# Block-sparse attention followed by a Fourier mixing layer: q and k of the later head pairs turned by VectorE instead of TensorE, with a new order of steps

## The chip, the cores and the metric

One core of one Trainium2 chip runs the whole program. A core has five engines that run side by side, each with its own queue of instructions that it works off strictly in order: TensorE (PE; its weight loads are listed apart as PEld), VectorE (DVE), ScalarE (ACT), GpSimd (POOL) and SyncE (SP). SP issues most of the DMAs, which sixteen DMA engines carry out. Engines wait for each other through semaphores. TensorE writes its results to PSUM, and DVE or ACT bring them to SBUF; GpSimd works only on SBUF here.

The metric is the device time of one execution in microseconds (us), as the median of several runs. A profile is of one execution.

## The reference

For each of 4 batches, 8 heads, 768 positions and head size 64, the program computes an attention in which a query sees its own block of 64 keys and the three blocks whose mean key scores highest, and of these only keys at or before it. The heads are laid side by side to 768 x 512, and a Fourier mixing layer and a two-layer network with W1 (512 x 2048) and W2 (2048 x 512) follow.

```python
k_rep = k.reshape(B, H, n_blocks, block, D).mean(axis=3)          # block 64, 12 blocks
gate_scores = np.einsum('bhsd,bhnd->bhsn', q, k_rep)
gate_scores = np.where(causal, gate_scores, -1000000000.0)
top_idx = np.argsort(gate_scores, axis=-1)[..., -top_k:]          # top_k 3
# mask: the chosen blocks and the query's own block, key position <= query position
scores = scale * np.matmul(q, k.transpose(0, 1, 3, 2))
attn = softmax(np.where(mask, scores, -1000000000.0))
x = np.matmul(attn, v)                                            # then (B, S, H * D)

mixed = np.real(np.fft.fft(np.fft.fft(x, axis=1), axis=2))
u = x + mixed
un = (u - mean(u)) / np.sqrt(var(u) + 1e-06)
out = u + np.maximum(un @ w_ch1, 0.0) @ w_ch2
```

All inputs and the output are float32.

## The kernel before

Two heads make a head pair, P = 0 to 15, four to a batch. A pair's q and k are needed with the head dimension on the partitions: 64 rows of the one head above 64 rows of the other, 768 positions along the free dimension. In DRAM a head is 768 rows of 64 floats. `load` (L264) brings it to SBUF with positions on the partitions, as a tile `nat` of 128 x 6 x 2 x 64, and `a_tp` (L286) lets TensorE transpose the six 128 x 128 blocks into PSUM as the tile `tp`. From there `a_sums` (L294) adds k over blocks of 64, `a_k` (L304) casts k to f16 for the scores, and `a_q32` (L313) copies q to a float32 tile in SBUF.

The code is a set of small steps, and the order in which they are issued is written out as one long list, ORDER (L112 to L179), with each step as name:arguments. The instructions of an engine stand in its queue exactly as their steps stand in this list. The place of a step beside steps of *other* engines has no force of its own: there, only data and buffers make one wait for another. The steps, with their engines:

| step | engine | what |
|---|---|---|
| Lk, Lq, Lv : P | SP | loads of k, q, v of pair P; v is cast to f16 by vc : P (POOL) |
| tk, tq : P | PE | six transposes of k, of q, into `tp` (L292) |
| ks, kh : P | DVE | sums of k by block (L297); the same, kept apart by head |
| kc : P; qc : P; qs : P | ACT; DVE; POOL | k to f16 (two instructions from pair 7 on, L311); q to SBUF (L316); q to f16 (two, L225) |
| g : P | PE | gate scores (L342), from the float32 q and the sums of k |
| gt, gx, gl, gm : P | DVE | gate scores turned (L354), the highest found, compared, and turned back (L386) |
| K : P | POOL | the choice of blocks, as 32 more rows below q (8 instructions, L225, and a memset up to pair 9) |
| s : P,i; e : P,i; d : P,i | PE; ACT; POOL | scores of piece i (L414); exp (L431); the diagonal blocks cut (L437) |
| v : P; x : P | PE; DVE | 42 matmuls with v (L449); divided by the sum, into the batch's `x` |
| fs, fd, f : b or P | DVE | additions that halve the Fourier transform |
| y; ty, tr; m : b | PE; ACT, DVE; PE | Fourier transform along positions (L519), copies out of PSUM, then along the features (L552) |
| u, bn, nv; xu; nr : b | DVE; ACT; POOL | x + mixed, its statistics; centring; the inverse root (12 small instructions) |
| xt, un (batch 0); un (others) | PE, DVE; SP | transposes of the centred rows to `unT`, later by transposing DMAs (L593) |
| w : b,i; r : b,i | PE; ACT, DVE for every fourth i | one of 16 column blocks of W1: eight matmuls (L629, L631); relu (L641, L639) |
| c : b,st,h; o; od | PE; DVE; SP | W2, half of the sum for 128 rows (L656; L648 for the last 128 rows, in halves of 256 columns); added to u (L668); store (L673) |
| W, X; Li, LF, LT, Lc | POOL; SP | loads of W1 in three parts, of W2 in two (X:0, X:1); constants |

The work of one batch's mixing layer is laid beside the attention of the next. "The first W1 product" is the step w of batch 0 that comes first.

Three pools set more waits. PSUM is cut into four buffers of two banks (`pst`, L215); every PE step that makes a new result takes one, and has to wait until the result before it in that buffer has been read. `nat` has three buffers each for q and k, so the load of pair P waits until pair P-3 has been read. The f16 q and k (`qk`) have three slots.

The functions that the diff touches, and what calls them:

Of the kernel before, what the change touches and what calls it, by code (L numbers as in the profile page):

```python
# [183 lines left out]
def kernel(  # L184
# [101 lines left out]
    def a_tp(P, who):  # L286
# [4 lines left out]
        for st in range(NST):  # L291
            nc.tensor.transpose(ps[:, 128 * st:128 * st + 128], src[:, st, :], id32)  # L292
# [495 lines left out]
```

## Time and profile before

| | |
|---|---|
| median of 3 runs | 298.1 us (298.1, 298.16, 297.7) |
| span of the profiled execution, first to last instruction | 295.6 us |
| busy in the span: PE, PEld | 286.5, 180.2 us |
| busy in the span: DVE, ACT, POOL | 192.5, 164.2, 111.1 us |
| DMA packets, data | 93200, 33.53 MB |

The whole time of the profiled execution is not on record apart from its span; the runs beside it took 2.1 to 2.6 us more than that span. Busy time is the time in which an engine has an instruction in work. PE works on several matmuls at once, so the duration of one (a 128 x 512 matmul has a mean of 379 ns) is longer than the time from one to the next; the chain that ended last shows the latter. In rows of groups, `out<-in` names tiles, then come the shapes, the count, the busy time and the mean duration of one in ns, and the idle time of the engine just before them. In the step names used here, the profile's `tp` rows on PE are tk and tq, `h` rows are w, `c` rows are c, `sc` are s, `av` are v.

### The profile page before, as it was taken

The page shows a single profiled execution, that of the slowest core. Times are in us where ns is not written, and L with a number is a line of the kernel's source. Part 1 is how long each engine was busy: PE and PEld are TensorE (multiplying, and loading weights), DVE is VectorE, ACT ScalarE, POOL GpSimd, SP SyncE. Part 2 cuts the span into 40 slices and gives each one's busy share as a digit, 9 for nine tenths or more (in the row PEclk, how much of TensorE's full clock was granted, in tenths as well). Part 3 has the DMA queues.
Part 4 walks back from the last instruction along what each step waited for, and adds up shares of the span by engine and source line. Part 5 has one row for each costly group of instructions (what it writes and reads, how often), then busy time and mean ns, then how long its engine had stood idle before and what let it go on. Part 6 is the DMA issues. An engine that isn't in the chain of part 4 may idle for free.

```text
span 295.6 us, 6738 instructions
## 1 busy us (share of the span) xinstructions
PE 286.5 (97%) x2633; PEld 180.2 (61%) x2633; DVE 192.5 (65%) x597; ACT 164.2 (56%) x205; POOL 111.1 (38%) x286
## 2 busy tenths in 40 slices
PE   8899999999999999999999999999999999999995
...
GB/s 197 268 228 230 262 245 199 195 230 118 226 185 211 168 55 186 118 164 176 3 0 2 0 9 136 38 72 71 2 1 2 32 103 44 142 0 2 0 91 125
DMA packets 93200, 33.53 MB, mean 113 GB/s; under 512 B 85936, under 2 KB 89968, under 8 KB 93168
## 3 DMA queue, kind: packets, MB, share of 16 engines
q1 hardware_dynamic: 87504, 28.47, 40.6%
...
q10 hardware_dynamic: 2000, 0.44, 0.7%
...
q14 instruction: 11, 0.09, 0.1%
...
## 4 chain that ended last, share of the span: by engine, by line
PE 84%; DVE 7%; ACT 6%; DMA 1%; issue 1%; DVEq 0%; ACTq 0%
PE c L656 26%; PE h L629 19%; PE h L631 10%; PE sc L414 7%; PE av L449 6%; ACT pt L431 5%; PE tp L292 5%; PE yp L519 2%; PE mx L552 2%; DVE q L316 2%; PE mx L553 1%; PE warmps L693 1%; DVE u L566 1%; PE g L342 1%; PE c L648 1%; PE sc L409 1%
## 5 line engine op out<-in xcount | busy, mean ns | idle before, releaser
L431 ACT ACTIVATE pt<-sc 128x1024 f16<-128x1024 f32 (+1 forms) x96 | 83.3, 923 | 26.6 <-PE sc L414 19.7
L629 PE MATMUL h<-unT,w 128*128 128x512 f16 x256 | 85.1, 379 | 0.0
L656 PE MATMUL c<-w_sb,hT 128*128 128x512 f16 x368 | 83.8, 379 | 0.0
L631 PE MATMUL h<-unT,w 128*128 128x256 f16 x256 | 69.7, 272 | 0.4 <-DMA unT<-x 0.4
L641 ACT ACTIVATE hT<-h 128x768 f16<-128x768 f32 x48 | 37.8, 813 | 43.7 <-PE h L631 43.7
L656 PEld LDWEIGHTS <-hT 128*128 128x128 f16 x368 | 35.6, 98 | 39.3 <-issue 0.5
L437 POOL TENSOR_SCALAR_AFFINE_SELECT pt<-pt 128x256 f16<-128x256 f16 x96 | 37.5, 414 | 58.5 <-ACT pt L431 57.6
L629 PEld LDWEIGHTS <-w 128*128 128x128 f16 x256 | 25.0, 97 | 29.2 <-issue 1.3
L668 DVE SCALAR_TENSOR_TENSOR u<-c,rs,u 128x512 f32<-128x512 f32 (+1 forms) x25 | 17.5, 725 | 31.2 <-PE c L656 30.4
L639 DVE TENSOR_SCALAR hT<-h 128x768 f16<-128x768 f32 x16 | 15.3, 955 | 29.7 <-PE h L631 29.6
L578 ACT ACTIVATE x<-u,nm 128x512 f16<-128x512 f32 x24 | 15.9, 715 | 22.5 <-DVE nm L572 22.3
L292 PE MATMUL tp<-id,nat 128*128 128x128 f32 x192 | 27.5, 284 | 0.6 <-ACT pt L431 0.3
L631 PEld LDWEIGHTS <-w 128*128 128x128 f16 x256 | 25.0, 98 | 4.3
L225 POOL TENSOR_SCALAR_AFFINE_SELECT qk<-mt 32x160 f16<-32x160 f16 x72 | 23.1, 341 | 10.8 <-DVE mt L386 9.1
L414 PE MATMUL sc<-qk 96*128 96x512 f16 (+3 forms) x144 | 26.8, 305 | 0.0
L225 POOL TENSOR_SCALAR_AFFINE_SELECT qk<-q 64x768 f16<-64x768 f32 (+1 forms) x25 | 20.6, 825 | 14.8 <-DVE q L316 14.1
L292 PEld LDWEIGHTS tp<-id,nat 128*128 128x128 f32 x192 | 22.2, 146 | 5.7 <-issue 1.6
L449 PE MATMUL av<-v,pt 128*128 128x65 f16 x672 | 23.0, 193 | 0.1
L449 PEld LDWEIGHTS <-pt 128*128 128x128 f16 x672 | 22.0, 97 | 1.7 <-POOL pt L437 0.5
L297 DVE TENSOR_REDUCE kr<-tp 128x12 f32<-128x768 f32 x16 | 15.1, 945 | 5.9 <-PE tp L292 5.9
L222 POOL TENSOR_TENSOR t<-vr,rs 128x6 f32<-128x6 f32 x12 | 2.4, 199 | 43.5 <-DVE rs L609 42.9
L414 PEld LDWEIGHTS <-qk 96*128 96x128 f16 x144 | 13.3, 97 | 8.9 <-issue 0.5
...
## 6 DMA issues: line engine op xcount, KB each, us to landing
...
w_sb<-in_moe_w_ch_dram POOLq DMA_DIRECT2D x2, 1024.0 KB, 10.2
...
```

The lines of the kernel that those rows point to most:

```text
L225: nc.gpsimd.affine_select(out=out, in_=in_, pattern=[[0, i] for i in n], base=0, channel_multiplier=0, compare_op=ALU.is_ge, fill=0.0)
L292: nc.tensor.transpose(ps[:, 128 * st:128 * st + 128], src[:, st, :], id32)
L414: nc.tensor.matmul(ps[:, e, co:co + q1 - q0], qk[0:96, e, 1, 128 * jt:128 * jt + 128], qk[0:96, e, 0, q0:q1], start=True, stop=True)
L431: nc.scalar.activation(out=d["pt"][:, o:o + 2 * n].rearrange("p (e c) -> p e c", e=2), in_=d["sc", i][:, :, 0:n], func=AF.Exp, scale=0.125)
L437: nc.gpsimd.affine_select(out=dg, in_=dg, pattern=[[0, 2], [1, 128]], base=0, channel_multiplier=-1, compare_op=ALU.is_ge, fill=0.0)
L449: nc.tensor.matmul(av[:, e, 66 * st:66 * st + 65], pt[:, co:co + 128], vv[:, e, jt, 0:65], start=(cnt == 0), stop=(cnt == 20))
L578: nc.scalar.activation(out=x_b[:, 2 * kp + k2, :], in_=u_b[:, k2, :], func=AF.Identity, scale=0.0625, bias=nm[:, k2:k2 + 1])
L629: nc.tensor.matmul(hp[:, 0:512], w1s, unT[:, dt, 0:512], start=(dt == 0), stop=(dt == NDT - 1))
L631: nc.tensor.matmul(hp[:, 512:768], w1s, unT[:, dt, 512:768], start=(dt == 0), stop=(dt == NDT - 1))
L641: nc.scalar.activation(out=hT, in_=hp, func=AF.Relu)
L656: nc.tensor.matmul(c_ps[b, g[0]][:, st - g[0], :], h_t[b, it][:, 128 * st:128 * (st + 1)], w2_sb[:, it, :], start=(it == 0), stop=(it == N ...
L668: nc.vector.scalar_tensor_tensor(out=o, in0=ps, scalar=st_t[b][1][:, st:st + 1], in1=o, op0=ALU.mult, op1=ALU.add)
```

## The change

For q of pairs 7 to 15 and k of pairs 9 to 15 (`BLK`), the load cuts the head into blocks of 32 positions by 32 features. Four DMAs, one for each head and half of its features, put 32 partitions each: partition r of a group holds position r of each of the 24 blocks, and along the free dimension come the 24 blocks with their 32 features. A DMA's runs are 128 bytes where they were 256. VectorE's 32 x 32 block transpose of that tile, 128 x 768 float32, is then the layout that TensorE made. For q the transpose takes the place of the copy in `a_q32` (qc). For k it is a new step, kb (`k_turn`), which turns the tile in place; `a_sums` and `a_k` then read that SBUF tile. The steps tk:9 to tk:15 and tq:7 to tq:15 are gone, with the PSUM tiles that they wrote, and kb:9 to kb:15 are added.

From w:0 on, the list has a new order: which block of W1 comes when, how scores, W1 and W2 steps alternate on PE, and the queues of ACT, DVE, POOL and SP. Up to there only tq:8 and tq:7 are taken out, and the loads have their new form.

```diff
@@ ORDER @@
...
-e:5,4 m:0,0 u:0,1 xu:0,2 d:5,4 tk:8 d:5,1 d:4,2 u:0,0 xu:0,1 d:5,0 xt:0,2 W:2 g:6 un:0,2 xu:0,0
-xt:0,1 gt:6 tq:8 un:0,1 kc:8 xt:0,0 qc:8 tq:7 un:0,0 qs:8 v:4 Lq:10 Lk:10 Lv:6 Lq:11 qc:7 bn:0,3
-w:0,4 d:5,3 qs:7 bn:0,1 w:0,5 r:0,4 gx:6 ks:8 w:0,6 r:0,5 gl:6,0 kh:7 gl:6,1 x:4 w:0,7 r:0,6 gm:6
-w:0,3 r:0,7 s:6,5 r:0,3 s:6,1 e:6,5 s:6,3 e:6,1 kh:8 s:6,2 fs:4,0 bn:0,4 w:0,2 e:6,2 d:6,1 X:0
-e:6,3 g:7 w:0,0 d:6,5 gt:7 r:0,2 d:6,3 vc:6 gx:7 s:6,4 r:0,0 vc:5 s:6,0 e:6,4 tk:9 Li:0 gl:7,0
-Lv:7 tq:9 gl:7,1 e:6,0 gm:7 w:0,11 Lq:12 Lv:8 K:7 qc:9 kc:9 g:8 r:0,11 v:5 gt:8 d:6,0 ks:9 w:0,8
-qs:9 gx:8 w:0,10 x:5 r:0,8 d:6,4 d:6,2 gl:8,0 s:7,5 s:7,2 r:0,10 kh:9 fs:4,1 w:0,1 bn:0,5 e:7,5
-vc:7 e:7,2 tq:10 gl:8,1 Lv:9 r:0,1 X:1 gm:8 s:7,4 qc:10 w:0,15 d:7,2 e:7,4 K:8 bn:0,0 g:9 r:0,15
-s:7,0 w:0,9 gt:9 e:7,0 gx:9 vc:8 tq:11 r:0,9 d:7,0 Lv:10 s:7,1 qc:11 d:7,5 tk:10 d:7,4 e:7,1
-gl:9,0 s:7,3 ks:10 v:6 e:7,3 kh:10 gl:9,1 kc:10 gm:9 d:7,3 s:8,4 bn:0,2 d:7,1 w:0,12 vc:9 x:6
...
-r:3,12 r:3,9 r:3,14 c:3,0,0 w:3,15 c:3,4,0 r:3,15 c:3,1,0 c:3,0,1 c:3,1,1 c:3,5,0 o:3,0 od:3,0
-o:3,1 c:3,3,0 od:3,1 o:3,5 od:3,5 c:3,4,1 c:3,2,1 o:3,4 od:3,4 c:3,3,1 c:3,5,1 o:3,3 od:3,3 o:3,2
-od:3,2 o:3,6 od:3,6
...
+tr:0,0 s:5,3 d:5,2 s:5,4 d:4,3 kh:6 W:1 ty:0,0 m:0,2 qs:6 e:5,3 u:0,2 m:0,1 vc:4 e:5,4 m:0,0 u:0,1
+xu:0,2 d:5,4 tk:8 d:5,1 d:4,2 u:0,0 xu:0,1 d:5,0 xt:0,2 W:2 g:6 un:0,2 xu:0,0 xt:0,1 gt:6 un:0,1
+kc:8 xt:0,0 qc:8 un:0,0 qs:8 v:4 Lq:10 Lk:10 Lv:6 Lq:11 qc:7 bn:0,3 gx:6 w:0,1 gl:6,0 r:0,1 w:0,2
+gl:6,1 gm:6 r:0,2 w:0,5 s:6,0 s:6,3 w:0,6 ks:8 kh:7 x:4 kh:8 bn:0,4 g:8 g:7 fs:4,1 s:6,1 r:0,5 e:6,0
+e:6,3 r:0,6 gt:7 s:6,4 gx:7 gl:7,0 e:6,4 w:0,0 gt:8 e:6,1 kb:9 ks:9 gl:7,1 gm:7 bn:0,1 r:0,0 w:0,12
+r:0,12 w:0,7 r:0,7 s:6,5 s:6,2 w:0,13 r:0,13 e:6,5 w:0,10 w:0,4 w:0,3 e:6,2 qc:10 gx:8 kb:10 ks:10
+kh:10 qc:9 d:6,1 d:6,4 d:6,0 qs:7 K:7 vc:5 d:6,2 X:0 d:5,3 Li:0 Lv:7 Lq:12 Lv:8 Lv:9 s:7,5 r:0,3
+r:0,4 v:5 x:5 s:7,0 r:0,10 w:0,14 kh:9 gl:8,0 g:9 e:7,5 g:10 e:7,0 gt:9 r:0,14 w:0,8 bn:0,5 gl:8,1
+gm:8 gx:9 fs:5,1 gl:9,0 s:7,4 w:0,15 kc:9 r:0,8 gl:9,1 fs:5,0 gt:10 s:7,3 e:7,4 e:7,3 r:0,15 s:7,1
+e:7,1 w:0,11 r:0,11 gm:9 bn:0,0 bn:0,2 nv:0 s:7,2 kc:10 e:7,2 d:7,5 d:7,0 vc:6 vc:7 K:8 qs:9 d:6,5
+d:6,3 d:7,4 X:1 d:7,1 d:7,2 d:7,3 vc:8 K:9 vc:9 nr:0 Lv:10 Lv:11 Lk:11 w:0,9 r:0,9 v:6 fs:4,0 s:8,4
+s:8,3 x:6 c:0,2,0 c:0,3,0 s:8,1 v:7 c:0,0,0 e:8,4 fs:6,0 x:7 s:8,0 s:9,2 c:0,1,0 s:9,4 c:0,3,1
+fs:6,1 gx:10 fd:6,1 gl:10,0 fd:6,0 gl:10,1 fs:7,1 gm:10 fs:7,0 fd:7,1 fd:7,0 f:1,1 f:1,3 s:8,5 o:0,3
+e:8,3 c:0,1,1 e:8,1 f:1,2 qc:11 o:0,1 s:9,3 e:8,0 e:9,2 s:9,5 c:0,2,1 e:9,4 c:0,0,1 e:8,5 e:9,3
+y:1,1 kb:11 f:1,0 ks:11 kh:11 g:11 y:1,0 e:9,5 o:0,2 s:9,0 o:0,0 ty:1,1 tr:1,1 s:8,2 c:0,4,0 gt:11
+s:9,1 ty:1,0 e:8,2 e:9,0 tr:1,0 m:1,1 Lq:13 od:0,1 Lq:14 od:0,2 od:0,0 Lk:12 Lk:13 qc:12 gx:11
+gl:11,0 gl:11,1 gm:11 u:1,1 e:9,1 m:1,0 u:1,0 m:1,2 kc:11 xu:1,1 xu:1,0 d:8,5 d:8,0 vc:10 vc:11
+d:8,3 qs:10 K:10 d:8,4 d:8,1 qs:11 d:9,4 d:9,2 d:9,5 d:8,2 d:9,0 d:9,1 d:9,3 qs:12 pg:1 K:11 u:1,2
+v:8 v:9 x:8 c:0,5,0 c:0,5,1 xu:1,2 kb:12 s:11,5 s:11,1 e:11,1 x:9 s:10,1 ks:12 kh:12 qc:14 e:10,1
+o:0,5 c:0,4,1 s:10,0 o:0,4 g:12 e:11,5 gt:12 s:11,0 s:10,4 s:11,3 gx:12 bn:1,3 fs:9,0 kb:13 ks:13
+un:1,1 un:1,0 un:1,2 Lk:14 od:0,4 Lv:12 od:0,3 Lv:13 od:0,5 Lk:15 Lq:15 w:1,1 s:10,2 w:1,10 w:1,2
+e:10,0 e:11,0 e:10,4 s:10,3 e:11,3 s:10,5 e:10,2 w:1,11 r:1,10 w:1,8 kh:13 bn:1,0 bn:1,4 kb:14
+gl:12,0 gl:12,1 r:1,1 r:1,2 r:1,11 s:11,4 w:1,7 ks:14 kh:14 qc:13 e:10,3 g:14 kc:13 e:10,5 g:13
+w:1,4 r:1,8 r:1,7 gm:12 e:11,4 kc:12 s:11,2 gt:13 gx:13 gl:13,0 w:1,9 e:11,2 gt:14 w:1,6 fs:8,1
+gx:14 gl:13,1 gm:13 d:10,0 d:10,5 d:10,4 d:10,3 K:12 d:11,0 d:10,2 d:10,1 d:11,3 qs:13 d:11,4 d:11,2
+vc:13 d:11,1 d:11,5 K:13 gl:14,0 r:1,4 v:10 s:12,5 w:1,5 s:12,3 r:1,9 x:10 gl:14,1 r:1,6 w:1,14
+r:1,5 s:12,0 e:12,5 v:11 s:12,2 e:12,3 e:12,0 w:1,0 s:13,2 w:1,3 x:11 kb:15 fs:11,1 fs:8,0 w:1,15
+fs:10,1 fs:9,1 r:1,3 r:1,14 s:13,5 r:1,0 r:1,15 bn:1,1 bn:1,5 fs:10,0 bn:1,2 e:13,2 s:12,1 e:12,2
+w:1,12 s:12,4 e:12,1 w:1,13 r:1,12 kc:15 c:1,0,0 e:13,5 r:1,13 c:1,0,1 s:13,4 s:13,0 e:13,0 c:1,1,0
+fd:10,0 fs:11,0 fd:11,1 fd:11,0 gm:14 fd:10,1 f:2,1 ks:15 kh:15 qc:15 f:2,3 f:2,2 f:2,0 nv:1 e:13,4
+s:13,3 e:13,3 c:1,1,1 s:13,1 e:13,1 e:12,4 d:12,3 d:12,5 K:14 nr:1 d:12,4 d:13,2 d:13,5 qs:14 d:12,2
+qs:15 vc:12 d:12,1 d:13,0 d:13,1 d:13,3 d:12,0 c:1,4,0 o:1,1 y:2,0 tr:2,0 y:2,1 c:1,5,0 o:1,0 g:15
+ty:2,1 tr:2,1 m:2,2 ty:2,0 m:2,0 m:2,1 c:1,4,1 v:12 gt:15 u:2,0 u:2,1 u:2,2 c:1,2,0 c:1,5,1 gx:15
+gl:15,0 gl:15,1 gm:15 kc:14 xu:2,2 xu:2,0 xu:2,1 od:1,1 od:1,0 Lv:14 un:2,2 Lv:15 un:2,1 un:2,0 pg:2
+K:15 d:13,4 s:14,3 o:1,4 e:14,3 c:1,3,0 s:14,0 e:14,0 s:14,4 v:13 s:15,3 c:1,3,1 e:15,3 s:15,0
+s:14,5 s:15,5 e:14,4 e:15,5 c:1,2,1 s:14,2 w:2,3 s:14,1 x:12 o:1,5 e:14,5 s:15,4 bn:2,3 s:15,2
+bn:2,1 bn:2,0 w:2,4 e:15,0 e:14,2 w:2,9 e:15,4 s:15,1 e:15,2 w:2,7 x:13 w:2,2 w:2,1 r:2,4 fs:13,1
+o:1,2 e:14,1 e:15,1 o:1,3 w:2,12 fs:12,1 r:2,3 bn:2,4 bn:2,5 fs:12,0 bn:2,2 nv:2 d:15,0 d:14,2
+d:15,5 d:15,3 d:15,4 vc:15 d:14,5 d:14,3 d:14,0 nr:2 d:14,4 d:15,2 d:15,1 vc:14 d:14,1 v:15 x:15
+r:2,9 r:2,1 v:14 w:2,0 fs:15,0 fs:15,1 w:2,13 w:2,15 x:14 fs:14,0 fs:13,0 r:2,15 w:2,8 r:2,12 w:2,5
+w:2,6 r:2,2 w:2,11 w:2,10 r:2,0 fd:15,1 r:2,7 fs:14,1 fd:14,0 r:2,8 r:2,11 fd:15,0 fd:14,1 f:3,1
+f:3,2 r:2,5 r:2,6 w:2,14 f:3,3 c:2,0,0 r:2,14 r:2,10 c:2,1,0 y:3,1 r:2,13 c:2,0,1 c:2,1,1 tr:3,1
+f:3,0 o:2,0 ty:3,1 y:3,0 ty:3,0 c:2,4,0 tr:3,0 m:3,1 m:3,0 c:2,5,0 m:3,2 c:2,2,0 c:2,2,1 o:2,1 u:3,0
+u:3,1 u:3,2 c:2,4,1 c:2,5,1 bn:3,2 o:2,5 o:2,2 c:2,3,0 c:2,3,1 bn:3,3 bn:3,0 od:1,3 od:1,5 od:2,0
+od:1,2 od:2,1 od:1,4 xu:3,0 xu:3,1 xu:3,2 un:3,0 un:3,2 un:3,1 w:3,15 w:3,4 w:3,14 o:2,3 w:3,6 w:3,2
+r:3,14 w:3,5 w:3,10 r:3,4 r:3,6 o:2,4 r:3,15 bn:3,5 r:3,5 bn:3,1 w:3,0 w:3,8 w:3,7 bn:3,4 r:3,7
+w:3,1 r:3,2 r:3,0 r:3,1 w:3,11 w:3,3 r:3,3 r:3,8 w:3,12 r:3,12 r:3,10 w:3,9 r:3,9 w:3,13 r:3,13
+r:3,11 nv:3 c:3,5,0 c:3,5,1 c:3,0,0 nr:3 pg:3 c:3,1,0 c:3,0,1 c:3,1,1 o:3,0 c:3,2,0 c:3,2,1 o:3,5
+c:3,4,0 c:3,4,1 o:3,6 c:3,3,0 o:3,1 o:3,2 o:3,4 c:3,3,1 o:3,3 od:3,1 od:3,5 od:2,5 od:2,2 od:3,0
+od:2,4 od:2,3 od:3,2 od:3,6 od:3,4 od:3,3
@@ -202,6 +200,7 @@
     NSLOT = 3
     NVS = 4
     NX = 7
+    BLK = (range(7, NPAIR), range(9, NPAIR))
 
     C = _consts_np()
     dr = {n: nc.inline_tensor(C[n], name=f"c_{n}") for n in C}
@@ -258,7 +257,7 @@
 
 
     nat = {}
-    pairs = [{} for _ in range(NPAIR)]
+    pairs = [{"slot": P % NSLOT} for P in range(NPAIR)]
     x_t, u_t, un_t, h_t, st_t = {}, {}, {}, {}, {}
 
     def load(P, who):
@@ -271,10 +270,17 @@
             nat[P, 2] = t
             return
         t = apool.tile([128, NST, 2, 64], FP, tag=f"nat{who}", name=f"nat{who}_{P}", bufs=3)
+        nat[P, who] = t
+        if P in BLK[who]:
+            nat[P, who] = t = t.rearrange("p st e d -> p (st e d)")
+            for g in range(4):
+                eng.dma_start(t[32 * g:32 * g + 32].rearrange("p (n c) -> p n c", c=32),
+                              src[b, 2 * hp + g // 2, :, 32 * (g % 2):32 * (g % 2) + 32]
+                              .rearrange("(n r) c -> r n c", r=32))
+            return
         for e in range(2):
             eng.dma_start(t[:, :, e, :],
                           src[b, 2 * hp + e].rearrange("(st p) d -> p st d", p=128))
-        nat[P, who] = t
 
     def v_cast(P):
         pcopy(v_s[P % NVS][:, :, :, 0:64].rearrange("p e st d -> p (e st) d"), nat[P, 2],
@@ -285,11 +291,14 @@
 
     def a_tp(P, who):
         d = pairs[P]
-        d["slot"] = P % NSLOT
         d["tp", who] = ps = pst([128, S], f"tp{who}_{P}")
         src = nat[P, who].rearrange("p st e d -> p st (e d)")
         for st in range(NST):
             nc.tensor.transpose(ps[:, 128 * st:128 * st + 128], src[:, st, :], id32)
+
+    def k_turn(P):
+        pairs[P]["tp", 1] = t = nat[P, 1]
+        nc.vector.transpose(out=t, in_=t)
 
     def a_sums(P):
         ps = pairs[P]["tp", 1]
@@ -313,7 +322,10 @@
     def a_q32(P):
         q32 = apool.tile([128, S], FP, tag="q32", name=f"q32_{P}")
         pairs[P]["q32"] = q32
-        nc.vector.tensor_copy(out=q32, in_=pairs[P]["tp", 0])
+        if P in BLK[0]:
+            nc.vector.transpose(out=q32, in_=nat[P, 0])
+        else:
+            nc.vector.tensor_copy(out=q32, in_=pairs[P]["tp", 0])
 
     def a_q(P):
         q32, qk = pairs[P]["q32"], qk_s[P % NSLOT]
@@ -737,7 +749,7 @@
         "LT": lambda _: nc.sync.dma_start(fs_sb, dr["FS"].ap()),
         "LF": lambda _: nc.sync.dma_start(fd_sb, dr["FD"].ap()), "Lc": lambda _: consts_next(), "Li": lambda _: ind_slot0(),
         "W": load_w1, "X": load_w2, "iz": blocks,
-        "tk": lambda P: a_tp(P, 1), "tq": lambda P: a_tp(P, 0), "ks": a_sums, "kh": a_half,
+        "tk": lambda P: a_tp(P, 1), "tq": lambda P: a_tp(P, 0), "kb": k_turn, "ks": a_sums, "kh": a_half,
         "kc": a_k, "qc": a_q32, "qs": a_q,
         "g": g_mm, "gt": g_turn, "gx": g_max, "gl": g_less, "gm": g_back, "K": stage_K,
         "s": s_mm, "e": s_exp, "d": s_sel, "vc": v_cast,
```

## The prediction

> **What bounds the kernel now.** I read the granted clock first, then the busy table by stage, PE's own waits, the chain that ended last, and last the rows by shape that price each edit. The busy table has the columns stretch, length, then busy microseconds of PE, PEld, DVE, ACT and POOL, clock, DMA share, GB/s.
>
> ```profile
> core 0: 295.6 us, clock 1.000
> 58.60:100.00 41.40, 41.40 (x423) 26.34 (x420) 35.12 (x137) 29.34 (x36) 24.14 (x53) 1.00 1.02 199
> 100.00:145.00 45.00, 44.62 (x372) 27.98 (x371) 31.95 (x105) 27.38 (x35) 27.25 (x71) 1.00 0.52 121
> 145.00:190.00 45.00, 45.00 (x439) 29.31 (x437) 34.74 (x104) 26.95 (x35) 19.50 (x51) 1.00 0.13 29
> ```
>
> From 58.6 us, where the first W1 product w:0 starts, PE is never free. The waits of PE between 58.6 and 292 us are this one line:
>
> ```profile
> PE h L631 <- DMA unT<-x: 0.4, 1, 0.4
> ```
>
> The chain confirms it: PE's own steps follow each other to the end.
>
> ```profile
> 106.02 0.66 PE tp L292 x6
> 240.21 8.63 PE c L656 x40
> 283.48 6.91 PE c L656 x32
> 290.39 1.76 PE c L648 x16
> 292.17 0.48 DVE u L668
> ```
>
> Forty matmuls of 512 columns in 8.63 us are 0.216 us each, one behind the other, so from 58.6 us on an instruction taken from PE is worth its full issue time, as long as everything else is on time. Before 58.6 us DVE and ACT lead. A w step (eight matmuls) is 1.30 us, a c step 1.73, v 1.28, g 0.41, m 0.87, an s step 0.11 to 0.44.
>
> The rows that price the edit (operation, shapes, count | busy, mean ns | idle before):
>
> ```profile
> L316 DVE COPY q<-tp 128x768 f32<-128x768 f32 x16 | 15.1, 945 | 3.6 <-PE tp L292 3.5
> L349 DVE STREAM_TRANSPOSE gt<-g 128x288 f32<-128x288 f32 x7 | 3.3, 473 | 0.0
> L354 DVE STREAM_TRANSPOSE gt<-g 128x160 f32<-128x160 f32 x9 | 3.1, 346 | 3.5 <-PE g L342 3.4
> L727 POOL DMA_DIRECT2D w_sb<-in_moe_w_ch_dram x2 | 1.8, 896 | 0.0
> q1 hardware_dynamic: 87504, 28.47, 40.6%
> w_sb<-in_moe_w_ch_dram POOLq DMA_DIRECT2D x2, 1024.0 KB, 10.2
> ```
>
> **1. PE loses 16 groups of six transposes.** Fourteen (k and q of pairs 9 to 15) stand in the saturated part. One group is 0.66 us in the chain: 14 x 0.66 = 9.2 us gone. The other two, tq:8 and tq:7, ran at 55.17 and 56.37, around xt:0,0 and ahead of v:4 and w:0. Without them xt:0,0 still waits for the ACT step xu:0,0, which ended at 55.89; 55.9 + 0.45 + v:4 1.28 = 57.7, and un:0,0 on DVE ends at 57.77 as before. So w:0 starts at 57.8 instead of 58.6: 0.8 us.
>
> **2. DVE gets seven k turns (kb); nine q copies become turns.** No row has a 128x768 block transpose. The two f32 rows give (473-346)/128 = 0.99 ns a column, so 473 + 480 x 0.99 = 948 ns. The upper bound is the shortest row scaled, 346 x 768/160 = 1661 ns; the lower one is the slope alone, 760 ns. I take 0.95 us: both rows lie on that line, and the copy it replaces, of the same shape, is 945 ns. So q changes nothing and k adds 7 x 0.95 = 6.7 us. Between 58.6 and 190 us DVE has 101.8 us of work in 131.4; it will have 108.5 in about 126, 86%. That hides the turns on average, not everywhere (part 4). If a turn costs 1.66 us, 16 x 0.71 = 11.4 us more come, and DVE is at 95%.
>
> The Trainium skill speaks against this edit ("VectorE: DVE Perf Modes", Rules for kernel authors: take TensorE for a 128x128 transpose where PSUM will do) and states 311 ns for the DVE and 390 ns for the TensorE one (The three transpose paths). By its figures a 768-column turn would be an estimated 1.87 us, and 84 transposes on PE 32.8 us. The rows decide: streamed, PE needs 0.11 us for one.
>
> The sums (ks) and the cast (kc) of k read SBUF instead of PSUM, at the 945 and 792 ns of their PSUM rows; I expect no change, within 0.1 us each. What vanishes with the PSUM result is a buffer held from the transpose to the cast, sixteen times.
>
> **3. Loads.** Each of 16 loads becomes four DMAs of 128-byte runs: 3072 packets for 1536. Queue q1's mean packet is 0.406 x 295.6 x 16 / 87504 = 21.9 ns. If half a run costs half, nothing is added; if it costs the same, 1536 x 21.9 / 16 = 2.1 us a load. The trace's packet records lie between: 18 ns for 256 bytes, 11 ns for 64, so about 13 ns for 128, or 0.8 us a load. Four issues cost SP about 2.2 us instead of 1.1. Cover: k9 and q9 still arrive before 58 us; of the later ones k10 lands some 4 us ahead of kb:10 and k14, behind un:1 on SP, 3 us ahead of kb:14. I cost it at 0. If the cover is gone, a load late by 3 us holds DVE and then the scores behind it.
>
> "DMA: Bandwidth & Descriptors" (Why small descriptors are slow) gives about three cycles of overhead a packet beside one per 32 bytes. Its figures make 7 cycles for 11, an estimated 0.5 us a load, between the same ends.
>
> **4. The new order.** I followed each engine's list through the built program, step by step with the rows above, and with the PSUM buffer that each PE step takes over (there are four). The PE steps from w:0,1 on sum to 222.4 us without waits. The waits I find, on the new run's clock:
> - v:5, 0.9 us. It needs d:5,3, which moved on POOL from ahead of qs:7 to behind K:7, vc:5, d:6,2 and X:0. e:6,1 ends 3.25 us after s:6,1 starts (e:6,3, r:0,6 and e:6,4 are ahead of it on ACT). Then come three d 1.1, qs:7 1.7, K:7 3.1, vc:5 0.9, d:6,2 0.4, X:0 0.9, d:5,3 0.4: 11.8 us in all. PE's work from s:6,1 to v:5 is seven w and four s, 10.6, and 0.3 of waits.
> - g:10, 0.6. It takes w:0,14's buffer; only g:9 (0.41) stands between, and r:0,14 needs 0.81 plus 0.2 of hand-over.
> - s:10,1, 1.05. It takes the buffer of s:11,1, the step right ahead, so the whole of e:11,1 (1.03) lies open.
> - w:1,7, 0.75. Its buffer is s:10,5's, and e:10,5 stands on ACT behind e:10,3 (1.03) and kc:13 (1.6).
> - v:8 and v:9, 0.45. They take the buffers of m:1,1 and m:1,0; u:1,1 is on DVE behind qc:12, gx:11, gl:11 and gm:11 (2.6 us).
> - Six of 0.1 to 0.35, 1.5 together: s:6,4 (r:0,6 starts behind e:6,3), s:7,1 (gt:10 on DVE behind two fs and gl:9), w:1,11 (r:1,1 behind r:1,10), g:13 (e:11,4), v:12 (d:12,0 on POOL behind qs:14, qs:15 and vc:12) and s:14,0 (e:14,3 behind three xu steps).
>
> That is 5.25 us. The old 0.5 at w:1,11 (the line of waits above, and its hand-over) goes. Least is g:10 and s:10,1, 1.65, which no timing elsewhere removes; most is double, 10.5.
>
> Near misses, costed at 0: X:1 moves on POOL from 79.6 to about 89, lands 10.2 us later at 99.3, and c:0,3,1 needs it at 100.5. nr:1 stands ahead of twelve POOL steps that v:12 needs, and waits for nv:1 at the end of 15 us of unbroken DVE work. un:3 lands about 0.5 us ahead of w:3,15. Each can cost 0 to 2 us.
>
> **5. The tail.** It ended with a 256-column half, o:3,6 0.48 us and a 128 KB store that lands in 1.7. Now it ends with o:3,3, 0.75, and a 256 KB store, 2.1: 0.7 us more. Seven stores of batches 2 and 3 are put off to just behind o:3,1 on SP, but about 9 us before the end, at 0.35 us an issue; they drain in time.
>
> **Sum.** 295.6 - 9.2 - 0.8 - 0.5 + 5.25 + 0.7 = 291.0 us of span. The profiled execution has only its span on record; the median of the runs, 298.1, is 2.5 above it, and I carry that: 293.5 us, 1.5% faster.
>
> **Rivals.**
> - The waits mostly vanish. For: the sixteen freed PSUM holds, and POOL at 54% and DVE at 77% of that stretch before. Against: g:10 and s:10,1. 291.0 - 3.6 = 287.4, time 289.9; with none at all 285.8, time 288.3.
> - Slower: DVE becomes the bound between 58 and 180 us. One mechanism: a turn costs more than 0.95 us, by itself or because it and POOL hold each other up at SBUF. For: the fixed order leaves it no way round (kb:9 is ahead of gm:7, kb:11 of tr:1,1, kb:15 of nv:1), and a POOL d step, 0.41 us, was up to 0.68 beside DVE work. Against: the two rows on one line. At 1.66 us and all of it open, 291.0 + 11.4 = 302.4, time 304.9; half open 299.2. It turns the sign from 4.6 us on the path, 0.29 us a turn.
> - Slower by DMA: block loads of 32 partitions run at half the rate, k10, k11 and k14 come late. For: DMA share 1.02 up to 100 us. Against: the margins of part 3. Three loads at 2 to 3 us: about 300.
> - That the transposes are not gone is excluded: the built program has 96 left of 192.
>
> **Chances.** Forecast (291 to 297.4) 0.48, waits gone (288.3 to 291) 0.18, no change 0.05, DVE 0.20, DMA 0.09. A measurement of this kernel tells 0.2%, 0.6 us. So faster 0.66, same 0.05, slower 0.29. The range: its low end is the sum with no waits, rounded up; its high end takes in DVE half open and late loads and leaves out the worst, about 0.1; below it lie 0.04. 288.5 to 302.
>
> **What would show it.** tp x96, and tp gone from PE after 58 us. The new turn rows at about 950 ns. w:0,1 at 57.8. PE waits of about 5 us between 58 and 287, the longest at s:10,1 behind ACT and at v:5 behind POOL; DVE near 199 us. I am wrong if a turn takes over 1.2 us, if PE waits for DMA nat, or if the waits pass 10 us.

## The result, and the profile after

The changed kernel took 294.81 us (four executions, 294.79 to 294.87), the kernel before 297.9 beside it: a ratio of 0.9908, 95% interval 0.9886 to 0.9929. The forecast was 293.5. In a later comparison (experiment 5) four of six executions of the same kernel took 300.0 to 303.2 us, longer than all eleven of the kernel before beside them (297.21 to 299.41), and ratios leave such executions out.

The span went from 295.6 to 292.8 us. Core line and busy table of the changed kernel (stretch, length, busy us of PE, PEld, DVE, ACT, POOL, then clock, DMA share, GB/s):

```profile
core 0: 292.8 us, clock 0.999
58.60:100.00 41.40, 40.67 (x395) 24.11 (x394) 33.57 (x129) 27.50 (x33) 27.72 (x64) 1.00 1.07 179
100.00:145.00 45.00, 42.32 (x355) 25.21 (x353) 40.40 (x130) 30.80 (x39) 21.84 (x52) 1.00 0.69 137
145.00:190.00 45.00, 45.00 (x419) 27.90 (x418) 32.27 (x89) 27.08 (x35) 23.98 (x64) 1.00 0.24 42
```

PE is no longer busy without a gap, and between 100 and 145 us VectorE is busy 40.4 of 45 us. PE's waits from 57 us on (engine, line, what it waited for: total, times, longest) were one line of 0.4 us before; now:

```profile
PE c L668 <- DVE u L680: 2.6, 3, 1.5
PE sc L426 <- ACT pt L443: 1.2, 1, 1.2
PE av L461 <- DVE u L578: 1.0, 2, 0.5
PE g L354 <- ACT hT L653: 0.5, 1, 0.5
PE h L641 <- DVE unT L602: 0.2, 1, 0.2
PE h L641 <- ACT pt L443: 0.2, 1, 0.2
```

The rows of the edited work by group (count | busy us, mean ns of one | idle before), and the DMA queue of the loads (packets, MB, share):

```profile
L326 DVE STREAM_TRANSPOSE q<-nat 128x768 f32<-128x768 f32 x9 | 8.7, 967 | 0.0
L301 DVE STREAM_TRANSPOSE nat<-nat 128x768 f32<-128x768 f32 x7 | 6.8, 968 | 0.1
L306 DVE TENSOR_REDUCE kr<-nat 128x12 f32<-128x768 f32 x7 | 6.6, 946 | 0.1
L297 PE MATMUL tp<-id,nat 128*128 128x128 f32 x96 | 13.5, 281 | 0.8 <-DMA nat<-in_k_dram 0.3 <-ACT pt L443 0.3
q1 hardware_dynamic: 112592, 28.47, 45.6%
```

A turn is 0.97 us, 96 of 192 transposes are left, and the queue carries the same bytes in 25088 more packets.

The longest wait is one that the forecast did not have. The timeline of the changed kernel at the two W2 products that wait for VectorE (start, us, what, idle before it and who ended that):

```profile
241.15 1.41 DVE L680 SCALAR_TENSOR_TENSOR u<-c,rs,u 128x512 f32<-128x512 f32 x2 [2.47 <-PE c L668]
242.62 1.24 PE L668 MATMUL c<-w_sb,hT 128*128 128x512 f16 x5 [1.50 <-DVE u L680]
...
286.10 1.41 DVE L680 SCALAR_TENSOR_TENSOR u<-c,rs,u 128x512 f32<-128x512 f32 x2 [6.34 <-PE c L668]
286.90 1.46 PE L668 MATMUL c<-w_sb,hT 128*128 128x512 f16 x6 [0.84 <-DVE u L680]
```

VectorE waits for PE, does two residual steps, and only then PE goes on. `w2_mm` puts two row tiles into one PSUM tile (sets 0-1, 2-3, 4-5; in batch 3 only 0-1 and 2-3). c:2,3,0 stands in the list behind o:2,2, which reads the other half of that tile, and so it waits for it; o:2,2 is on VectorE behind o:2,5, and that waits for c:2,5,1, the product just ended. At c:3,3,1 it is the same with o:3,2, which was listed behind c:3,3,0 and waits for that.

### The profile page after: what moved, and what is told of

Same layout as the page of the kernel before. It is cut to its first block, busy times and chain, and to the rows that moved or that the text cites. A ratio compares the mean times of both kernels' runs of the same rounds, so it can differ in the third digit from the quotient of the medians.

```text
span 292.8 us, 6583 instructions
## 1 busy us (share of the span) xinstructions
PE 276.4 (94%) x2537; PEld 169.1 (58%) x2537; DVE 198.3 (68%) x604; ACT 164.1 (56%) x205; POOL 113.2 (39%) x286
## 4 chain that ended last, share of the span: by engine, by line
PE 63%; DVE 16%; ACT 8%; SPq 6%; DMA 3%; issue 2%; POOL 0%; DVEq 0%; ACTq 0%; POOLq 0%
PE c L668 21%; PE h L641 15%; PE h L643 8%; ACT pt L443 5%; SPq L277 5%; PE sc L426 5%; PE av L461 4%; DVE kr L306 2%; PE yp L531 2%; DVE u L680 2%; DVE q L328 2%; DMA nat<-in_q_dram 1%; PE warmps L705 1%; DVE u L578 1%; PE c L660 1%
## 5 line engine op out<-in xcount | busy, mean ns | idle before, releaser
L426 PE MATMUL sc<-qk 96*128 96x128 f16 (+3 forms) x144 | 26.8, 306 | 1.2 <-ACT pt L443 1.2
L578 DVE SCALAR_TENSOR_TENSOR u<-mx,x 128x512 f32<-128x512 f32 x24 | 15.6, 685 | 4.3 <-PE mx L565 2.5
L610 DVE BATCH_NORM_STATS2 bst<-u 128x6 f32<-128x512 f32 x24 | 16.1, 670 | 0.0
L421 PE MATMUL sc<-qk 64*128 64x512 f16 (+3 forms) x112 | 14.6, 306 | 1.5 <-ACT pt L443 0.8
```

Source lines behind the costliest of these rows:

```text
L426: nc.tensor.matmul(ps[:, e, co:co + q1 - q0], qk[0:96, e, 1, 128 * jt:128 * jt + 128], qk[0:96, e, 0, q0:q1], start=True, stop=True)
L578: nc.vector.scalar_tensor_tensor(out=u_b[:, k2, :].rearrange("p (m two) -> p two m", two=2), in0=mps[:, k2, :].rearrange("p (two m) -> p t ...
L610: nc.vector.bn_stats(out=bst, in_=u_t[b, kt // 2][:, kt % 2, :])
```

## The experiments

The ratio beside each is to the kernel before in the same group of runs; groups ran on different chips.

### 1. The turns in the old order

```diff
@@ ORDER of before; tk:9 to tk:15 and tq:7 to tq:15 taken out, k turned ahead of its first reader @@
-... tk:9 ... kc:9 ... ks:9 ...
+... kb:9 kc:9 ... ks:9 ...
```

> The block loads and the VectorE turns alone, in the order of steps of before (each k turn listed just ahead of the first reader of k). Theory (the PE work that went is the gain, the new order pays for waits that it makes itself): the span of before 295.6 less 14 x 0.66 = 9.2 us of PE work, plus some 2 to 5 us of hand-overs where PE steps now follow their producers more closely: span 288.5 to 291.5, time 291 to 294, so no slower than the changed kernel's 294.8. Rival (the new order is what makes the turns pay; in the old one VectorE is late in places where it had PE's transposes as cover): over 296.

Measured: 308.64 us (307.2 to 309.7), ratio 1.035 (1.032 to 1.038); span 307.7, mean clock 0.972. PE's waits in this kernel, the largest:

```profile
PE av L461 <- POOL v L224: 10.0, 1, 10.0
PE h L643 <- DMA unT<-x: 5.3, 1, 5.3
PE h L641 <- DMA w<-in_moe_w_ch_dram: 1.4, 1, 1.4
```

The theory falls: the old order does not carry the change. But VectorE, which the rival named, is not what fails. All three waits are for transfers: the cast of v of pair 5 stood on GpSimd behind that of pair 6, which waited 11.53 us for its load. And while PE stood still its granted clock fell to 0.50, for 10.24 and 6.83 us.

### 2. The new order with q on TensorE

```diff
-    BLK = (range(7, NPAIR), range(9, NPAIR))
+    BLK = (range(0), range(9, NPAIR))
@@ ORDER: tq:P just ahead of qc:P, for P = 7 to 15 @@
-qc:8 un:0,0 ... qc:7 ... qc:10
+tq:8 qc:8 un:0,0 ... tq:7 qc:7 ... tq:10 qc:10
```

> The new order with k turned by VectorE, but q of the last nine pairs loaded and transposed as before (tq just ahead of each copy of q). VectorE's work is unchanged (a copy from PSUM in place of a turn, both about 0.95 us); PE has 9 x 6 = 54 transposes more, 9 x 0.66 = 5.9 us. Theory (PE is saturated from 57.8 us on, every group that went is worth its full 0.66): 294.8 + 5.9 = 300.7 us, 299 to 302. Rival (part of the transposes fills time in which PE would wait, 8.5 us of such waits are in the changed kernel): 296.5 to 298.

Measured: 310.1 us (308.7 to 311.2), ratio 1.040 (1.036 to 1.044); span 308.2. Both misjudged it. PE's waits, the largest:

```profile
PE c L668 <- DVE u L680: 4.1, 3, 1.8
PE av L461 <- DVE u L578: 2.4, 1, 2.4
PE h L641 <- DVE q L328: 1.0, 1, 1.0
```

The span is 15.4 us longer: 5.9 of transposes at the forecast's price, 6.4 more of PE waits (12.1 against 5.7), 1.7 of half clock, 0.5 of a longer tail (4.5 us behind the last matmul, not 4.0), some 0.9 not accounted for. The copy of q has the price of the turn (0.95), but it waits for PE, holds a PSUM buffer, and PE then waits for it: of seven lines of PE's waits that the changed kernel doesn't have, five are for `q`, 2.8 us together. So the turn gives more than its transposes: VectorE no longer follows PE there. How the other 3.6 us of added waits come about was not followed.

### 3 and 4. The unforeseen waits moved away

```diff
@@ ORDER, experiment 3 @@
-o:0,5 c:0,4,1    o:2,5 o:2,2 c:2,3,0 c:2,3,1 bn:3,3 bn:3,0    un:3,0 un:3,2 un:3,1
+c:0,4,1 o:0,5    o:2,5 c:2,3,0 c:2,3,1 bn:3,3 bn:3,0 o:2,2    un:3,0 un:3,1 un:3,2
-o:3,1 o:3,2 o:3,4 c:3,3,1 o:3,3
+o:3,1 o:3,4 c:3,3,1 o:3,2 o:3,3
@@ experiment 4: the same, and @@
-gl:11,0 gl:11,1 gm:11 u:1,1 e:9,1 m:1,0 u:1,0    x:9 s:10,1 ... o:0,5 c:0,4,1    g:9 e:7,5 g:10 ... w:0,8
+u:1,1 e:9,1 m:1,0 u:1,0 gl:11,0 gl:11,1 gm:11    x:9 c:0,4,1 s:10,1 ... o:0,5    g:9 e:7,5 w:0,8 g:10 ...
```

> Changed kernel with four entries of the list moved: the residual steps o:2,2, o:3,2 and o:0,5 behind the W2 products that use the other half of the same PSUM tile, and un:3,1 ahead of un:3,2. No work added or taken away. Theory (three PE waits of 1.66, 1.00 and 0.37 us exist only because an o that is listed ahead of a product of the same tile must be over first): 294.8 - 3.0 = 291.8 us, 291.2 to 292.5, and the waits of PE for u at the W2 products fall from 2.6 us to below 0.5. Rival (VectorE or the turned x of batch 3 is late anyway and PE waits at the next step): 294 to 295.

> The moves of the run before, and three more: u:1,1 and u:1,0 ahead of the three selection steps gl and gm of pair 11 on VectorE, the W2 product c:0,4,1 between the score products s:11,1 and s:10,1, and w:0,8 between g:9 and g:10. Theory (the waits of the changed kernel at c:2,3,0 1.66, c:3,3,1 1.00, c:0,4,1 0.37, v:8 and v:9 1.37, s:10,1 1.33, g:10 0.56 are hand-overs set by the list, each goes by itself): 294.8 - 6.3 = 288.5 us, 288 to 290. Rival (what one wait gives back, the next takes, since VectorE and ScalarE run only as far ahead as the four PSUM buffers let them): 291 to 293, as the moves of the run before alone, or above.

Measured: experiment 3 had one execution at 293.97 us, the other five at 299.8 to 304.1; experiment 4 one at 293.50, the others at 300.1 to 304.8. No ratio is to be had. What the moves did is read from step starts in the profiled executions (302.63 and 304.82 us), in stretches where the clock was 1.00; experiment 8 has the first three the same. From c:2,0,0 to c:2,3,0 it is 22.66 us where it was 24.33 (1.67 gained), from c:3,3,0 to c:3,3,1 1.73 where it was 2.73 (1.00 gained), and no PE wait for u at a c step is left in experiment 3. So the two waits were made by the list. But from the last matmul to the end it is 5.7 us instead of 4.0: o:3,2 now ran behind c:3,3,1 too, so 1.7 of the 2.7 was given back at the tail. Experiment 4 gained 0.7 at v:8 (g:11 to v:8 7.74 us, not 8.44), but nothing at s:10,1 (s:11,5 to w:1,1 7.07 us, 7.05 in experiment 3 and 6.67 in the changed kernel: PE's 1.17 us wait for exp moved to the next score step) and nothing at g:10 (v:5 to v:6 11.88 us, 11.78 before the move). Of the 6.3 us hoped for, then, 3.4 were hand-overs set by the list; at s:10,1 the rival was right.

### 5. The changed kernel once more

> The changed kernel itself, beside the other kernels of this group. In the runs of the c and o steps moved, one execution took 294.0 us and the others 300 to 304; their profile shows v of pair 7 landing 7.0 us late for its cast on GpSimd, a PE pause of 5.57 us behind it and the granted clock at 0.5 for about 6 us after that, in a stretch where the list was not touched. Theory (the changed kernel itself stands at the edge of its loads between 75 and 87 us): its executions fall on both sides too, some at 294.8, some at 300 to 304. Rival (the moved entries made it so): all at 294.5 to 295.5.

Measured, six executions in order: 302.55, 300.0, 302.23, 294.94, 303.22, 295.19; ratio of the two short ones 0.9892 (0.9856 to 0.9928). The theory holds: it takes no moved entries. The profiled execution here has a span of 300.5 us. Its waits of PE begin with the first line below; then the busy table at that place, and from its timeline the cast on GpSimd:

```profile
PE av L461 <- POOL pt L449: 5.5, 1, 5.5
```

```profile
88.00:90.00 2.00, 0.39 (x13) 0.26 (x9) 1.83 (x8) 1.76 (x3) 1.83 (x7) 1.00 0.90 185
92.00:94.00 2.00, 0.08 (x2) 0.09 (x3) 0.00 (x0) 0.00 (x0) 1.87 (x5) 0.50 0.11 20
96.00:98.00 2.00, 2.00 (x9) 0.88 (x7) 1.22 (x2) 1.44 (x2) 1.93 (x5) 0.50 0.79 101
```

```profile
87.28 0.90 POOL L224 TENSOR_SCALAR_AFFINE_SELECT v<-nat 128x768 f16<-128x768 f32 x1 [6.98 <-DMA nat<-in_v_dram]
```

The cast vc:7 waits 6.98 us for v of pair 7; d:6,5 and d:6,3 are behind it on GpSimd, and v:6 waits for them. PE stands for 5.5 us, and from 91.43 us the clock is 0.50 for 6.83 us, of which PE works 4.3 and so loses 2.2. 292.8 + 5.5 + 2.2 = 300.5.

Why is v late? Two issues meet here: Lv:7 on SP (`SPq` in a row is an issue on SP's queue) and X:0, the first 1 MB of W2, on GpSimd. Both follow the cast of v of pair 5, the first row: it frees the buffer that Lv:7 takes, and X:0 stands one d step behind it. First the execution with span 292.8, then the one with 300.5:

```profile
73.90 0.91 POOL L224 TENSOR_SCALAR_AFFINE_SELECT v<-nat 128x768 f16<-128x768 f32 x1
74.83 0.39 SPq L269 DMA_DIRECT2D nat<-in_v_dram  x1
75.10 0.90 POOL L739 DMA_DIRECT2D w_sb<-in_moe_w_ch_dram  x1
```

```profile
73.89 0.91 POOL L224 TENSOR_SCALAR_AFFINE_SELECT v<-nat 128x768 f16<-128x768 f32 x1
75.53 0.53 SPq L269 DMA_DIRECT2D nat<-in_v_dram  x1
75.10 0.90 POOL L739 DMA_DIRECT2D w_sb<-in_moe_w_ch_dram  x1
```

In the first, SP stood ready, and v is issued as the buffer comes free. 1486 of its 1536 packets go between 76 and 78 us, before W2's begin in earnest at 78, and v lands 4.0 us after its issue. In the second, SP was still busy with other loads, and v is issued 0.43 us *behind* W2; its packets go between W2's, about 150 in each us, and it lands after 11.7. The DMA queues of that execution between 80 and 84 us (packets, MB, share), W2's above that of v:

```profile
q0 software_dynamic: 591, 0.60, 90.8%
q1 hardware_dynamic: 598, 0.15, 28.7%
```

The two queues get the same number of packets, and since W2's have 1024 bytes and v's 256, v gets a fifth of the bytes. Over ten traced executions of kernels in the new order the order of the two issues has no exception: with Lv:7 ahead of X:0, by 0.06 to 0.27 us (six of them), v landed 3.6 to 5.6 us after its issue; behind it, by 0.35 to 0.61 us (three), after 11.6 to 12.4, and by 6.2 us (one), after 7.3. So 0.7 us on SP decide over 7.7. With this list the lead can't be more than the d step between the cast and X:0; in four of the six it is 0.27 us. That the order of these two issues causes it is read from these traces; moving X:0 alone was not tried.

### 6. The loads of before

```diff
         if P in BLK[who]:
-            ...
-            for g in range(4): ...
+            for e in range(2):
+                eng.dma_start(t[:, :, e, :],
+                              src[b, 2 * hp + e].rearrange("(st p) d -> p st d", p=128))
+            ...
```

> The changed kernel, but q and k of the block pairs loaded in the two DMAs of before (runs of 256 bytes, 1536 packets a load in place of 3072) and then turned by VectorE as in the changed kernel; the layout that VectorE turns is not that of the blocks, so that q and k of these pairs are permuted: left wrong, all durations kept. Theory (the block loads cost about 13.4 ns x 3072 less 18.1 ns x 1536 over 16 DMA engines = 0.84 us of DMA time each, hidden in the best executions): the best executions stay at 294.5 to 295, and the executions at 300 or above go. Rival (the loads have nothing to do with the late v): the same spread as the changed kernel has beside it. Second rival (the loads cost even the best executions something): below 294.

Measured: 294.07 us, four executions from 293.59 to 294.43; ratio 0.9853 (0.9824 to 0.9882). The changed kernel's best two beside it are 294.94 and 295.19, so some 1.0 us more, between the theory and the second rival. The two ratios' intervals overlap, and the profiled spans are 292.4 and 292.8: whether the block loads cost anything where v is in time is not clear of noise. None of four was over 295; by itself that is a hint only, but SP's wait in front of Lv:7 says why. First the changed kernel with span 292.8, then this one (what waited, for what: total, times, longest):

```profile
SPq L269 <- POOL v L224: 1.1, 1, 1.1
```

```profile
SPq L269 <- POOL v L224: 3.5, 1, 3.5
```

With the old loads SP is ready 3.5 us before the cast of pair 5 has freed the buffer; the block loads before it on SP leave 1.1 us of that, and in the execution with span 300.5 nothing. Lv:7 is issued 0.27 us ahead of X:0 here.

### 7. More work on VectorE

```diff
-            nc.vector.transpose(out=q32, in_=nat[P, 0])
+            for _ in range(2):
+                nc.vector.transpose(out=q32, in_=nat[P, 0])
```

> The changed kernel with every q turn issued twice in a row (the same result): 9 x 0.967 = 8.7 us more of VectorE, nothing else. Theory (PE sets the pace and VectorE at 68% has room, but each added turn pushes what is queued behind it on VectorE, so that a few hand-overs of 0.3 to 1.0 us grow): 295.5 to 298. Rival (VectorE is the bound in the pair stretches): 294.8 + 6 or more, over 301. Second rival (all hidden): 294.5 to 295.2.

Measured: 301.63 us (301.15 to 302.6), ratio 1.0115 (1.0091 to 1.014). 8.7 us of added turns cost 6.6 against the changed kernel's 294.94 and 295.19: 0.76 us for each us, and the time is 1.2% above the kernel before. PE's waits, three of them:

```profile
PE av L462 <- DVE u L579: 2.0, 1, 2.0
PE g L355 <- DVE krb L221: 1.8, 1, 1.8
PE h L642 <- DVE unT L603: 1.2, 1, 1.2
```

Against the changed kernel they grew by 3.9 us in all, and the pause of 2.04 us brought the clock to 0.50 for 3.41 us (1.7). The rival, VectorE as the bound, is nearer than the theory: a busy share of 68% over the span says nothing of a stretch at 40.4 of 45.

### 8. The moves that held, together

```diff
@@ ORDER: o:2,2 and un:3,2 as in 3, u:1,1 and u:1,0 as in 4, and @@
-c:3,2,1 o:3,5 c:3,4,0 ... c:3,3,0 o:3,1 o:3,2 o:3,4 c:3,3,1
+c:3,2,1 o:3,5 o:3,2 c:3,4,0 ... c:3,3,0 o:3,1 o:3,4 c:3,3,1
-vc:6 vc:7 K:8 qs:9 d:6,5 d:6,3 d:7,4
+vc:6 K:8 qs:9 d:6,5 d:6,3 vc:7 d:7,4
```

> The changed kernel with entries of the list moved, no work added or taken away: o:2,2 behind the two halves of c:2,3, un:3,1 ahead of un:3,2, o:3,2 ahead of c:3,4,0 and so of c:3,3,0 (not behind c:3,3,1, which cost 1.7 us at the end in the earlier run), u:1,1 and u:1,0 ahead of the selection steps of pair 11, and the cast of v of pair 7 on GpSimd four entries later, behind K:8 and d:6,3, so that a late v no longer holds the products of pair 6. Theory: 292.8 - 1.67 - 1.0 - 0.7 = 289.4 us of span, 291.4 us of time (291 to 292.5), and the executions at 300 or above go or come nearer. Rival (what these waits give back is taken by the next): 293.5 to 295.

Measured: 293.3 us (292.13 to 295.93, six executions), ratio 0.984 (0.980 to 0.988), 1.6% below the kernel before and 1.8 us below the changed kernel's 294.94 and 295.19, though the interval of their ratio, 0.9856 to 0.9928, touches this one. Core line and PE's waits:

```profile
core 0: 290.4 us, clock 0.998
```

```profile
PE sc L426 <- ACT pt L443: 1.2, 1, 1.2
PE c L668 <- DVE u L680: 0.9, 1, 0.9
PE g L354 <- ACT hT L653: 0.5, 1, 0.5
```

The waits sum to 3.3 us (5.7 before), and the span is 2.4 shorter, the same amount. The forecast of 289.4 for the span missed the wait at c:0,4,1, 0.86 us where the step had lost 0.37, and a tail 0.4 us longer (4.4 us behind the last matmul). No execution was over 296, but in the profiled one Lv:7 was ahead of X:0, so this alone doesn't show that the later cast is what helped; experiment 10 has that move by itself.

### 9. The old order with the loads of before

> The old order with the VectorE turns, as in the first run, but q and k of the block pairs loaded in the two DMAs of before; what VectorE turns is then not the block layout, so that q and k of these pairs are left permuted and wrong, all durations kept. In the first run PE waited 10.0 us for v of pairs 5 and 6, 5.3 us for the transposing DMAs of batch 1 and 1.4 us for W1, and the clock stood at 0.5 for 10.2 and 6.8 us. Theory (the old order failed on its loads alone, not on the turns): 307.7 - 16.7 - some 4 for the clock = 287 us of span, 289 to 291 of time, faster than the changed kernel. Rival (VectorE is late in the old order too, the loads only hid it): 295 to 300.

Measured: 296.47 us (294.1 to 297.0, and one at 302.1), ratio 0.9939 (0.9913 to 0.9966). With the loads of before the old order is 12 us better than in experiment 1, so the form of the loads is most of what it failed on; which part of it (shorter runs, four issues in place of two, 32 partitions a DMA) was not taken apart. It is not the 289 to 291 expected, and lies in the rival's range, but not for the rival's reason: what remains is again transfers:

```profile
PE h L642 <- DMA unT<-x: 3.4, 1, 3.4
PE h L640 <- DMA w<-in_moe_w_ch_dram: 1.9, 1, 1.9
```

No wait for VectorE exceeds 0.4 us. With the clock's 1.7, waits and clock are 8.2 us. Of the transposes, 9.2 us went behind the first W1 product and 1.0 ahead of it (PE was free for it at 57.6, not 58.6): 295.6 - 0.4 (the old wait) - 10.2 + 8.2 = 293.2. The span is 294.7, so 1.5 us went to delays too short for the list of waits.

### 10. The cast of v of pair 7 alone

```diff
-vc:6 vc:7 K:8 qs:9 d:6,5 d:6,3 d:7,4
+vc:6 K:8 qs:9 d:6,5 d:6,3 vc:7 d:7,4
```

> The changed kernel with one entry of the list moved: the cast of v of pair 7 on GpSimd from ahead of K:8 to behind d:6,3. Theory (the late v of pair 7 stops the products of pair 6 only because its cast stands ahead of d:6,5 and d:6,3 in GpSimd's queue): no execution has the PE pause of 5.5 us at v:6, and all take 294.5 to 296.5. Rival (v comes late whatever the queue order, and v:7 or X:1 takes the pause over): executions at 298 to 303 remain.

Measured, twelve executions: six at 294.7 to 295.4, six at 297.2 to 299.4. The profiled one has a span of 297.0. No pause of 5 us and no low clock is left in it, although v of pair 7 was issued 6 us behind X:0. But the rival has its share: the cast of pair 9 waits for its load with nr:0 behind it, and VectorE's first o of batch 0 for nr:0. GpSimd and VectorE in the timeline:

```profile
101.12 0.90 POOL L224 TENSOR_SCALAR_AFFINE_SELECT v<-nat 128x768 f16<-128x768 f32 x1 [4.61 <-DMA nat<-in_v_dram]
```

```profile
105.88 0.75 DVE L680 SCALAR_TENSOR_TENSOR u<-c,rs,u 128x512 f32<-128x512 f32 x1 [2.81 <-POOL rs L221]
```

Against 295, the kernel of experiment 5 lost 5 to 8 us in four executions, and this one loses 2 to 4.5 in six; the move does not take the cause away.

### 11. The old order, repaired by hand

```diff
-Lq:10 Lk:10 Lv:6 Lq:11    d:6,3 vc:6 ... vc:5 ... d:6,2       Lk:15 Lq:15 ... un:1,2    w:0,4 ... w:0,1
+Lv:6 Lq:10 Lk:10 Lq:11    d:6,3 ... vc:5 ... d:6,2 vc:6       un:1,2 Lk:15 Lq:15        w:0,1 ... w:0,4
```

> The old order with the VectorE turns and the block loads, correct, with a few entries moved so that loads are asked for in the order of need: the load of v of pair 6 ahead of q and k of pair 10, its cast behind d:6,2 in place of ahead of the cast of pair 5, k and q of pair 15 behind the last transposing DMA of batch 1, and column block 1 of W1 exchanged with block 4 (the first part of W1 lands first). Theory (the old order lacks nothing but the order of its loads): 287 to 291 us of span, 289 to 293 of time, level with or ahead of the best version so far at 293.3. Rival (other loads, k of pairs 11 to 14 above all, come late in turn, since an in-place k keeps its buffer until its cast): 296 or more.

Measured: 303.68 us (299.7 to 307.4), ratio 1.0156 (1.0108 to 1.0204). The three waits of experiment 1 are gone, but two others of 5.04 and 4.60 us have come, at scores that wait for K:8 and K:9: these stand on GpSimd behind the casts of v of pairs 7 and 9, which wait 8.94 and 4.26 us. The rival's kind of failure, by other loads than it named.

### 12. Loads and casts shifted once more

```diff
@@ ORDER of experiment 8 @@
-vc:7 d:7,4 X:1 d:7,1 d:7,2 d:7,3 vc:8 K:9 vc:9 nr:0
+X:1 vc:7 d:7,4 d:7,1 d:7,2 d:7,3 K:9 vc:8 nr:0 vc:9
```

> The version with moved entries that took 293.3 us, and three more moves on GpSimd: the load X:1 ahead of the cast of v of pair 7, the cast of v of pair 8 behind K:9, and the cast of v of pair 9 behind nr:0 (in the run with the cast of pair 7 alone, that of pair 9 waited 4.6 us for its load with nr:0 behind it, and the residual steps o of batch 0 were late). Theory (the executions above the best come from casts that wait for a late v with work of others behind them): nearly all executions at 292.1 to 293, the median at 292.5. Rival (the late loads themselves reach PE by q, k or W2, whatever the order on GpSimd): the same spread of 292 to 296 as before, median 293.3 or more.

Measured: 295.43 us (293.8 to 295.65, and one at 299.2), ratio 0.9898 (0.985 to 0.995): no gain over experiment 8. The later cast of pair 9 held its buffer, v of pair 11 waited for it on SP (four v issues, the first at 83.27, the last over at 101.69 us), k of pair 11 behind that, and g:11 1.45 us for k's sums. The theory falls: a cast put off holds its buffer, and the loads behind it wait.

## Why the prediction was right, and where it was wrong

One table carries most of it. From each profiled span are taken PE's waits from 57 us on as the profile lists them, and half of the time in which PE works at clock 0.50, but for the low stretch at the very end, where PE has no work.

| kernel | span | waits of PE | half clock | what is left |
|---|---|---|---|---|
| before | 295.6 | 0.4 | 0 | 295.2 |
| changed | 292.8 | 5.7 | 0 | 287.1 |
| changed, profile with late v (5) | 300.5 | 11.2 | 2.2 | 287.1 |
| moves (8) | 290.4 | 3.3 | 0 | 287.1 |
| cast of v7 (10) | 297.0 | 9.8 | 0 | 287.2 |
| 12 | 293.5 | 4.8 | 1.7 | 287.0 |
| old loads (6) | 292.4 | 5.5 | 0 | 286.9 |
| q turned twice (7) | 299.2 | 9.6 | 1.7 | 287.9 |
| q on TensorE (2) | 308.2 | 12.1 | 1.7 | 294.4 |
| turns, old order (1) | 307.7 | 18.2 | 4.1 | 285.4 |
| turns, old order, old loads (9) | 294.7 | 6.5 | 1.7 | 286.5 |
| turns, old order, repaired (11) | 301.6 | 11.8 | 4.2 | 285.6 |

In the new order, with each turn made once, what is left is the same within 0.3 us (286.9 to 287.2). Experiment 7 keeps 0.8 us that the list of waits does not explain, and in experiment 2 nine groups of transposes (5.9) are back. Experiments 3 and 4 are left out: their tail is 1.8 us longer, and in 4 the first W1 product starts 2.9 us later.

**PE's 9.2 us: right.** PE's busy time fell from 286.5 to 276.4 us for the sixteen groups. In the kernel before, the fourteen groups hold PE for 9.3 us, counted from the start of each to the next PE step. In the old order what is left goes from 295.2 to 285.4 to 286.5, that is 8.7 to 9.8 us for all sixteen groups, where the forecast had 9.2 and 0.8; about 1.0 of it lies ahead of the first W1 product. w:0,1 started at 57.77, forecast 57.8, with PE waiting its last 0.2 us for un:0,0 on VectorE.

**The turn: right in size, short in consequence.** 967 ns for a forecast 948, not the 1.87 us of the prediction's other estimate (by the two rows of the forecast, 346 ns for 160 columns and 473 for 288, 128 columns alone take some 0.31 us, and taking six times that counts the fixed part six times); VectorE at 198.3 us for 199; the sums of k at 946 ns. The rival "DVE becomes the bound" had a true mechanism: experiment 7 prices VectorE's time at 6.6/8.7 = 0.76. Nothing made a turn dearer, and so it did not happen. At that price the 3.1 us gained would be gone with some 0.25 us more a turn (3.1 / (16 x 0.76), an estimate), not 0.29: the price is lower than the forecast's, but so was the gain to lose.

**The loads at 0: wrong.** This is the step that failed in kind. The packet price was right: 128-byte packets took 13.3 ns on average in the profiled execution for "about 13", so 0.8 us a load. But the cover was judged by k10 and k14, by what waits for the block loads themselves. What they push back on SP, v of pair 7 and its race with W2, was not looked at. Experiment 6 puts it at some 1 us where v is in time, not clear of noise, experiment 5 at 5 to 8 us where it isn't, experiments 1 and 9 at 12 in the old order. The rival "slower by DMA", about 300 us with a chance of 0.09, named the right size and the wrong loads. So part of the hit is luck: the four executions that the forecast was compared with agree within 0.08 us, and in the profiled one of them v came in time. Of the six of experiment 5 four took 5 to 8 us more, as the one profiled with v late did, and the median of all six, 301.12 us, is above the kernel before (298.19).

**The waits: right in kind, 1.9 us too small.** Measured against the usual cost of each PE step (from its start to that of the next) they are 8.46 us instead of 5.25, and 1.79 of old ones went, not 0.5. Of the named ones g:10 was 0.56 (0.6), s:10,1 1.33 (1.05), v:8 with v:9 1.37 (0.45), w:1,7 0.32 (0.75). v:5 was forecast at 0.9 and cost nothing: d:5,3 ended at 76.43 as the sum had it, but v:5 began at 76.00, since only its sixteenth matmul reads what d:5,3 cuts, and it started at 76.49. The largest that were missed are c:2,3,0 1.66, c:3,3,1 1.00 and c:0,4,1 0.37. The forecast followed the four PSUM buffers from one result to the next; inside a buffer, two halves of one result share a tile, and that is where list place makes a wait. Experiments 3 and 8 show it for the first two.

**The tail: right,** 0.5 us for 0.7. **The sum:** 295.6 - 9.2 - 0.8 + (8.46 - 1.79) + 0.5 = 292.8, against 291.0 forecast; it closes because the waits are counted against the steps' usual costs. The median stands 2.0 over the span, not 2.5. So 1.8 us too little in the span, nearly all of it waits, and 0.5 too much in the offset make the 1.3 us between 293.5 and 294.81: the two errors partly cancel.
